# Two attentions and a soft mixture of experts on one core: one load stream through a byte ring, k turned on VectorE, second scores turned twice, and one written order for every part

## The chip, the cores and the metric

The kernel runs on one core of one Trainium2 chip, in fp32. The metric is the device time of one execution, in microseconds (us). A core has five engines that work side by side, each in the order of its own instructions: PE (TensorE, matmuls and transposes; its weight loads are shown apart, as PEld), DVE (VectorE), ACT (ScalarE), POOL (GpSimd) and SP (SyncE, which issues the transfers). Sixteen DMA engines carry the transfers between HBM and SBUF, the on-chip memory of 128 partitions. Matmuls write to PSUM, from where ACT or DVE copies.

## The reference

Eight batches, eight heads, 576 tokens, 64 values a head, and 32 packed queries `p` a head. Attention is done twice, then a soft mixture of eight experts with four slots each:

```
p_packed = softmax(scale * p @ k.T) @ v              # 32 x 64 for each batch and head
out      = softmax(scale * q @ p_packed.T) @ p_packed  # 576 x 64
x        = out as (4608 tokens, 512)
logits   = x @ phi                                   # 4608 x 32 slots
d = softmax of logits over the 4608 tokens;  slot_input = d.T @ x        # 32 x 512
slot_out[e] = relu(slot_input[e] @ w1[e]) @ w2[e]    # w1 512 x 1024, w2 1024 x 512
c = softmax of logits over the 32 slots;     result = c @ slot_out       # 4608 x 512
```

q, k and v are 9.4 MB each, the experts' weights 33.6 MB, the result 9.4 MB. The first-layer product of an expert needs slot inputs that depend on all tokens, so the experts come after the whole attention.

## The kernel before

**Steps.** The attention is cut into eight steps of two batches and four heads; two steps with the same batches make a duo. In a step `kp` (line 210) turns k on PE, 18 transposes of 128x128 into PSUM, copied to `kT` by `evac` (line 81, ACT or DVE, whichever has less to do by a running sum). `s1` (225) makes the scores of the packed queries, 16 matmuls that contract 64 rows, their maximum on DVE (247) and exponentials on ACT (251), which writes them with a stride of 18 elements so that keys 4p+j come together. `ap` (262) and `at` (277) turn these, `ppm` (285) multiplies with v, `ppn` normalises, `pt` (318) turns the packed values into `ppT`, `mp` (330) multiplies them with phi. `qp` (348) turns q, 18 transposes. `s2p` (367) makes the second scores with tokens on the partitions, 36 matmuls of 64 columns with q as the weights; `s2m`, `s2s` (386, 393) subtract the maximum on DVE, `e2` (424) is the exponential on ACT, `n2` (428) sums on DVE and scales on POOL, `a2p` (447) turns the result, `lg` (463) makes the logits. After each duo `f1` to `f4`, `gz`, `grg`, `gtg`, `gbg`, `gsg` (495 to 690) bring its share of the slot inputs to the running maximum.

**Order.** The loop at line 753 writes a turn by hand: step i to its scores, step i+1 to its packed keys. The last step and the last duo stand in a second hand-written order (line 867). Each engine follows its own instructions in that order.

**Loads.** All transfers go through SP's one queue. The big tiles of k, q, v and the weights share a pool of 15 places of 16 KB a partition (`NRING`); what does not fit lies in small tail tiles. k is loaded in rows of 4,096 bytes (line 111) and tails of 512 (112); q and v in rows of 1,024 bytes (121) and tails of 256 that go to 64 partitions (132). A w1 chunk is loaded by `load_w` (718) as two transfers of 512 KB, each to 64 of the 128 partitions, rows of 4,096 bytes (722, 723); a w2 chunk as one of 1 MB to all partitions, rows of 8,192 bytes (736). Pools for late weights open as attention tiles are given back (`extra`, `more`, `more2`, `more3`).

**Experts and result.** `layer1a` (line 978) runs four experts' first layers into one pair of banks in four column groups, `hidden` and `layer1b` turn the hidden units, `layer2` (1033) does the second layers (its matmul is line 1037), the last expert in halves of columns. The result is 36 matmuls of full contraction in fp32r (line 1150), copied by ACT and DVE, and written in 12 + 2 transfers.

## Time and profile before

| | |
|---|---|
| time, median of 3 runs | 259.22 us (255.44 to 261.7) |
| span of the profiled execution | 253.4 us |
| own time of the profiled execution, with what lies around the span | not listed apart; the fastest run is 2.0 us above the span, the median 5.8 us |
| busy PE, PEld, DVE, ACT, POOL | 200.2, 133.7, 119.7, 116.2, 25.0 us |
| mean granted clock of TensorE | 0.925 of full speed |
| bytes moved | 62.46 MB read, 9.44 MB written |

The span runs from the first to the last instruction. Busy time of PE is overlapped by its pipeline, so 145 us busy in 166 does not mean 145 us of columns. In the table by stretches each engine has its busy time and, in brackets, its instructions; PEclk is the granted clock as a share of full speed, and the DMA share is that of 16 engines.

### The profile page before, as it was taken

How to read it: one execution, taken by the hardware profiler on the slowest of the kernel's cores; microseconds unless marked ns; L12 is line 12 of the kernel's file. 1: busy time of each engine (PE TensorE's matmuls, PEld its weight loads, DVE VectorE, ACT ScalarE, POOL GpSimd, SP SyncE). 2: the span in 40 equal slices, each digit the busy share in tenths (PEclk: the TensorE clock that was granted, in tenths of full speed). 3: DMA queues.
4: the chain of work that ended last, by engine and by line, in shares of the span. 5: the costliest groups of instructions: out<-in, count | busy, mean ns of one | idle time of the engine just before them, and what ended most of it. 6: DMA issues, size and time to landing. Idle time of an engine off the chain costs nothing.

```text
span 253.4 us, 6754 instructions
## 1 busy us (share of the span) xinstructions
PE 200.2 (79%) x2843; PEld 133.7 (53%) x2843; DVE 119.7 (47%) x279; ACT 116.2 (46%) x253; POOL 25.0 (10%) x40
## 2 busy tenths in 40 slices
PE   1878899989979998879977976988462999989700
PEld 1556766756846866647845765754111433456300
DVE  2223463563853472785453535767710125168700
ACT  2385469577625669256658453451100200069700
POOL 3000003030030012021003003200020000000000
PEclk9999799999967999999999979899795899999965
DMA  5999999999999999999999999999999999039996
GB/s 153 304 312 278 320 285 301 260 319 291 294 308 313 320 303 288 241 239 262 284 256 240 244 235 349 420 341 208 223 229 290 398 416 379 21 109 398 419 411 156
DMA packets 41246, 72.33 MB, mean 285 GB/s; under 512 B 11392, under 2 KB 31104, under 8 KB 38400
## 3 DMA queue, kind: packets, MB, share of 16 engines
q1 hardware_dynamic: 41216, 71.90, 97.1%
q8 instruction: 22, 0.36, 0.6%
q14 instruction: 8, 0.07, 0.1%
HBM read 62.46 MB, written 9.44 MB: 284 GB/s over the span
## 4 chain that ended last, share of the span: by engine, by line
PE 54%; DMA 20%; ACT 12%; issue 5%; DVE 2%; SPq 1%; ACTq 0%
DMA w<-in_moe_w_dram 16%; PE s L380 7%; PE kp L220 7%; PE s L240 6%; PE so L1037 5%; PE hp L988 4%; PE m L294 4%; PE qp L361 4%; ACT a L251 4%; PE op L1150 2%; DMA k<-in_k_dram 2%; ACT kT L88 2%; ACT qT L88 2%; PE ap L269 2%; ACT a1T L88 2%
## 5 line engine op out<-in xcount | busy, mean ns | idle before, releaser
L88 ACT COPY kT<-kp 128x512 f32<-128x512 f32 (+1 forms) x42 | 19.1, 484 | 27.4 <-PE kp L220 27.4
L988 PE MATMUL hp<-w,xz 128*32 128x512 f32 x128 | 20.0, 675 | 10.9 <-DMA w<-in_moe_w_dram 10.4
L380 PE MATMUL s<-ppT,qT 128*64 128x64 f32 x576 | 22.6, 238 | 3.0 <-issue 1.9
L443 POOL TENSOR_TENSOR a<-a,z 128x1152 f32<-128x1152 f32 (+1 forms) x8 | 16.0, 1996 | 81.8 <-DVE z L442 62.3
L220 PE MATMUL kp<-ident,k 128*128 128x128 f32 x128 | 21.0, 307 | 3.6 <-issue 1.7
L380 PEld LDWEIGHTS s<-ppT,qT 128*64 128x64 f32 x576 | 20.2, 150 | 6.5 <-ACT qT L88 3.1
L88 ACT COPY qT<-qp 128x512 f32<-128x512 f32 (+1 forms) x40 | 20.3, 558 | 3.9 <-PE qp L361 3.4
L251 ACT ACTIVATE a<-s,nm 128x576 f32<-128x576 f32 x16 | 21.6, 1352 | 0.5 <-DVE nm L247 0.5
L220 PEld LDWEIGHTS kp<-ident,k 128*128 128x128 f32 x128 | 16.3, 157 | 8.8 <-issue 4.3
L247 DVE TENSOR_REDUCE nm<-s 128x1 f32<-128x576 f32 x16 | 12.0, 750 | 17.9 <-PE s L240 17.9
L390 DVE TENSOR_REDUCE mx<-s 128x16 f32<-128x512 f32 (+1 forms) x24 | 12.6, 555 | 16.2 <-PE s L380 16.1
L240 PE MATMUL s<-kT,pT 64*32 64x288 f32 x256 | 17.1, 446 | 3.8 <-ACT kT L88 3.3
L361 PE MATMUL qp<-ident,q 128*128 128x128 f32 x128 | 19.1, 286 | 0.9 <-issue 0.9
L88 ACT COPY a1T<-ap 128x512 f32<-128x512 f32 x16 | 8.7, 589 | 20.8 <-PE ap L269 20.8
L988 PEld LDWEIGHTS hp<-w,xz 128*32 128x32 f32 x128 | 6.4, 119 | 22.3 <-issue 21.4
L361 PEld LDWEIGHTS qp<-ident,q 128*128 128x128 f32 x128 | 16.0, 150 | 1.9 <-issue 1.9
L294 PE MATMUL m<-v,a1T 128*32 128x64 f32 x512 | 10.7, 232 | 4.5 <-issue 3.1
L435 DVE TENSOR_REDUCE z<-a 128x36 f32<-128x1152 f32 (+2 forms) x9 | 10.9, 1209 | 6.9 <-ACT a L426 6.2
L1037 PE MATMUL so<-w,hT 128*32 128x512 f32 x112 | 12.4, 592 | 0.0
L1005 ACT COPY hs<-hp 128x512 f32<-128x512 f32 x2 | 1.2, 586 | 24.4 <-PE hp L988 24.4
L294 PEld LDWEIGHTS m<-v,a1T 128*32 128x32 f32 x512 | 8.7, 116 | 6.6 <-issue 4.0
L1150 PE MATMUL op<-sh,cT 128*128 128x512 f32 x35 | 11.9, 444 | 0.2
(155 smaller groups left out, 321.3 us busy)
## 6 DMA issues: line engine op xcount, KB each, us to landing
w<-in_moe_w_dram SPq DMA_DIRECT2D x34, 512.0 KB, 16.4
w<-in_moe_w_dram SPq DMA_DIRECT2D x15, 1024.0 KB, 15.8
k<-in_k_dram SPq DMA_DIRECT2D x16, 512.0 KB, 6.7
q<-in_q_dram SPq DMA_DIRECT2D x16, 512.0 KB, 7.4
v<-in_v_dram SPq DMA_DIRECT2D x16, 512.0 KB, 8.0
out_dram<-ob SPq DMA_DIRECT2D x7, 1024.0 KB, 6.1
kx<-in_k_dram SPq DMA_DIRECT2D x16, 64.0 KB, 6.0
qx<-in_q_dram SPq DMA_DIRECT2D x16, 64.0 KB, 7.4
```

The lines of the kernel that those rows point to most:

```text
L88: nc.scalar.copy(dst, src)
L220: nc.tensor.transpose(tp[:, j * P : (j + 1) * P], src, ident)
L240: nc.tensor.matmul(ps[hs, x, 0:HALF], pTs[dd][xs, g, 4 * b2 + h].rearrange("p a s -> p (a s)"), kT[xs, :, hs], start=True, stop=True,)
L251: nc.scalar.activation(a1.rearrange("p (r t x) -> p x t r", t=T, x=2), ps[:, :, 0:HALF].rearrange("p x (t r) -> p x t r", t=T), AF.Exp, bi ...
L294: nc.tensor.matmul(s["m"][hs, b2 * D : (b2 + 1) * D], s["a1T"][:, 4 * b2 + j, hs] if j < 4 else a1tail[:, b2, hs], vm[:, b2, h, j * D : (j ...
L361: nc.tensor.transpose(tp[:, j * P : (j + 1) * P], qf[:, o : o + P], ident)
L380: nc.tensor.matmul(ps[us, j * 64 : j * 64 + 64], s["qT"][:, 8 * c + j, us], w, start=True, stop=True)
L390: nc.vector.tensor_reduce(mx, s[f"s2{c}"], axis=AX.X, op=ALU.max)
L443: eng.tensor_tensor(a2, a2, z2.unsqueeze(3).broadcast_to([P, nt, 4, NS]), op=ALU.mult)
L988: nc.tensor.matmul(hp[nh][32 * a : 32 * a + 32, :], xzf[:, (4 * e + a) * NSLOT : (4 * e + a + 1) * NSLOT], w1s[e, a // 2][:, a % 2, nh * 5 ...
L1037: nc.tensor.matmul(so[32 * a : 32 * a + 32, :], hTf[:, (NJ * e + j) * NSLOT : (NJ * e + j + 1) * NSLOT], w2s[e, j // 4][:, j % 4, :], star ...
L1150: nc.tensor.matmul(op, cT[:, o, :], sh, start=True, stop=True)
```

## The change

The kernel function is written anew. These parts matter:

- **Loads.** One list of transfers in the order of use, p, k, q, v of all steps, then w1, then w2, goes through one SBUF ring of 112 KB a partition, handed out in bytes. `release` is called after the last reader of a region is written, and `pump` then issues every next transfer that fits. k, q and v come as half steps of 590 KB to all 128 partitions, in rows of nine tokens, 2,304 bytes, without tails. w1 chunks are 1 MB to all 128 partitions, rows of 4,096 bytes. Seven weight chunks go into the attention's work space (`f_late`) and one into the space of the last probabilities (`f_lx`).
- **k** is turned by VectorE in 32x32 blocks, four transposes of 128x576 a step, and the first scores contract 32 rows at a time in a 4x4 tiling, 16 groups in four banks.
- **First softmax.** The exponentials are written with 32 contiguous elements; the product with v contracts 64 rows into 64 columns.
- **Second scores** are made with the packed keys as weights and q moving, so that the slots lie on the partitions; they are copied to SBUF and turned back by nine transposes a step (`st`); then maximum, subtraction in eight parts, exponential, sum on POOL (VectorE for the last step), scale.
- **The duo's share** is summed in column groups, `gr` in four, with tokens 64 at a time.
- **Result.** The slot shares stay in fp32, four tokens' slots side by side, and 36 matmuls contract 32 rows each.
- **Order.** Every part of the attention is one word of `ORDER`, 638 words, with its PSUM bank and the engine of its copy; the words `w` are matmuls of ones.

```diff
-NRING = 15
-NEXTRA = (2, 2, 2, 1, 1)
-NTAIL = 6
-NKTAIL = 3
-NAHEAD = 3
+RING = 28 * 4096
+NEXT = (3, 2, 2)
+ORDER = """
+p.0.0 w.4.0@0 w.1.0@0 px.0.0@4 kt.0.0 pc.0.0:a kt.0.1 kt.0.2
+kt.0.3 w.4.0@0 w.4.0@0 w.1.0@0 s1.0.0@0 s1.0.1 qp.0.0@7 mx1.0.0
+qp.0.2@6 qc.0.0:a qp.0.4@5 qp.0.3@4 qc.0.2:a qp.0.5@7 qc.0.4:v e1.0.0
...
+"""
...
-    def load_k(i):
-        dd, g = divmod(i, NG)
-        main = ring.tile([P, 2, 16 * D], F32, tag="ring", name=f"k_{i}")
-        tail = kpool.tile([P, 2, 2 * D], F32, tag="tail", bufs=NKTAIL, name=f"kx_{i}")
-        for b2 in range(2):
-            xs = k[2 * dd + b2, 4 * g : 4 * g + 4].rearrange("h (r t) d -> (h r) (t d)", r=32)
-            nc.sync.dma_start(out=main[:, b2], in_=xs[:, 0 : 16 * D])
-            nc.sync.dma_start(out=tail[:, b2], in_=xs[:, 16 * D : 18 * D])
-        kts[i] = (main, tail)
...
-        dd, g = divmod(i, NG)
-        main = ring.tile([P, 2, 4, TB * D], F32, tag="ring", name=f"{name}_{i}")
-        for b2 in range(2):
-            xs = src[2 * dd + b2, 4 * g : 4 * g + 4]
-            nc.sync.dma_start(
-                out=main[:, b2],
-                in_=xs[:, 0 : TB * P, :].rearrange("h (p j) d -> p h (j d)", j=TB),
-            )
-        return main
...
+    def region(key, width):
+        off = state["off"]
+        if off + width > RING // 4:
+            off = 0
+        state["off"] = off + width
+        return [key, off, width]
...
+    def pump():
+        while state["next"] < len(loads):
+            key, width, src = loads[state["next"]]
+            if key == "phi":
+                nc.sync.dma_start(out=width, in_=src)
+                state["next"] += 1
+                continue
+            if "at" not in state:
+                state["at"] = region(key, width)
+            _, off, _ = state["at"]
+            if not free(off, width):
+                return
+            regions.append(state.pop("at"))
+            where[key] = (off, width)
+            load(ring[:, off : off + width], src)
+            state["next"] += 1
...
+    def release(key, users=1):
+        left[key] = left.get(key, users) - 1
+        if left[key]:
+            return
+        for x in regions:
+            if x[0] == key:
+                regions.remove(x)
+                break
+        pump()
...
+    def rows9(src, i, b2):
+        dd, g = divmod(i, NG)
+        s = src[2 * dd + b2, 4 * g : 4 * g + 4]
+        return s.rearrange("(m x) (r t) d -> (x r) m (t d)", m=2, t=T)
...
+    for i in range(NSTEP):
+        for b2 in range(2):
+            loads.append((f"k{i}.{b2}", 2 * T * D, rows9(k, i, b2)))
...
+        for b2 in range(2):
+            loads.append((f"q{i}.{b2}", 2 * T * D, rows9(q, i, b2)))
+        for b2 in range(2):
+            loads.append((f"v{i}.{b2}", 2 * T * D, rows9(v, i, b2)))
...
+    def rows_w1(e, g):
+        return w1[e, 2 * P * g : 2 * P * (g + 1)].rearrange("(j p) f -> p j f", j=2)
+    LX = (3, 1)
+    for e in range(E):
+        for g in range(NG):
+            if (e, g) != LX:
+                loads.append((f"w1_{e}_{g}", 2 * FF, rows_w1(e, g)))
+    for e in range(E):
...
-    w1s, w2s = {}, {}
-    chunks = [(lay, e, c) for lay in (1, 2) for e in range(E) for c in range(2)]
-    def load_w(pool, lay, e, c):
-        n = f"w{lay}_{e}_{c}"
-            t = pool.tile([P, 2, FF], F32, tag="ring", name=n)
-            for g in range(NG):
-                nc.sync.dma_start(
-                    out=t[64 * g : 64 * g + 64],
-                    in_=w1[e, g * 4 * D : (g + 1) * 4 * D].rearrange("(h d) f -> d h f", d=D)[
-                        :, 2 * c : 2 * c + 2
-                    ],
-                )
...
-        for t0, nt in ((0, 4), (4, 4), (8, 1)):
-            tp = bank(pstr, f"kp_{i}_{b2}_{t0}")
-            for j in range(nt):
-                t = t0 + j
-                src = main[:, b2, t * P : (t + 1) * P] if t < 8 else tail[:, b2]
-                nc.tensor.transpose(tp[:, j * P : (j + 1) * P], src, ident)
-            evac(kT[:, t0 : t0 + nt].rearrange("p t x -> p (t x)"), tp[:, 0 : nt * P])
+    def f_kt(i, j, bank, eng):
+        b2, c = divmod(j, 2)
+        nc.vector.transpose(
+            kT[:, b2, :, c].rearrange("p m (t r) -> p m t r", t=T),
+            view(f"k{i}.{b2}").rearrange("p (m t c d) -> p m t c d", m=2, t=T, c=2)[:, :, :, c],
+        )
+        release(f"k{i}.{b2}", 2)
...
+    def f_s1(i, j, bank, eng):
+        dd, g = divmod(i, NG)
+        c = j
+        for y in range(4):
+            b2, m = y // 2, 1 - y % 2
+            for z in range(4):
+                rs = slice(32 * z, 32 * z + 32)
+                nc.tensor.matmul(
+                    ps[32 * y : 32 * y + 32, z, 0 : 32 * T],
+                    pT[rs, dd, b2, g, c, m],
+                    kT[rs, b2, m, c],
+                    start=(c == 0),
+                    stop=(c == 1),
+                )
...
+    def f_e1(i, x, bank, eng):
+        nc.scalar.activation(
+            a1[:, :, x].rearrange("p t (h r) -> p h t r", h=2),
+            s1v[:, x].rearrange("p h (t r) -> p h t r", t=T),
+            AF.Exp,
+            bias=nms[i % 2][:, x : x + 1],
+            scale=1.0,
+            accum_out=rzs[i % 2][:, x : x + 1],
+        )
...
+    def f_m(i, j, bank, eng):
+        if j == 0:
+            banks["m", i] = bank
+        b = banks["m", i]
+        for t in range(*tk(j)):
+            for b2 in range(2):
+                for x in range(2):
+                    rs = slice(64 * x, 64 * x + 64)
+                    nc.tensor.matmul(
+                        ps[64 * b2 : 64 * b2 + 64, b + x, 0:P].rearrange("p (m d) -> p m d", m=2),
+                        a1T[rs, t, b2],
+                        view(f"v{i}.{b2}").rearrange("p (m t d) -> p m t d", m=2, t=T)[rs, :, t],
+                        start=(t == 0),
+                        stop=(t == T - 1),
+                    )
+        release(f"v{i}.0", 3)
+        release(f"v{i}.1", 3)
...
+    def f_s2(i, j, bank, eng):
+        if j == 1:
+            banks["s2", i, 1] = bank
+            for b2 in range(2):
+                for x in range(2):
+                    nc.tensor.matmul(
+                        ps[64 * x : 64 * x + 64, bank, R * b2 : R * b2 + R],
+                        ppTs[i % 2][:, x, b2, 1:3].rearrange("p v s -> p (v s)"),
+                        qT[:, b2, 4, 64 * x : 64 * x + 64],
+                        start=True,
+                        stop=True,
+                    )
+            return
...
+        b2 = j // 2
+        for x in range(2):
+            for m in range(2):
+                n0, n1 = nk(2 * m)
+                for u in range(2):
+                    us = slice(64 * u, 64 * u + 64)
+                    a = 2 * x + (u + m) % 2
+                    nc.tensor.matmul(
+                        ps[
+                            32 * a : 32 * a + 32,
+                            banks["s2", i, 2 * u],
+                            4 * R * b2 : 4 * R * b2 + 4 * R,
+                        ].rearrange("p (n r) -> p n r", n=4),
+                        ppTs[i % 2][us, x, b2, 2 * (1 - m) + u],
+                        qT[us, b2, n0:n1, 64 * x : 64 * x + 64],
+                        start=True,
+                        stop=True,
+                    )
...
+    def f_st(i, j, bank, eng):
+        n0, n1 = nk(j)
+        for n in range(n0, n1):
+            o = (n - n0) * P
+            nc.tensor.transpose(
+                ps[:, bank, o : o + P], s2T[:, n].rearrange("p b r -> p (b r)"), ident
+            )
+        banks["st", i, j] = bank
...
+    def f_mx2(i, j, bank, eng):
+        n0, n1 = nk(j)
+        nc.vector.tensor_reduce(
+            mxs[i % 2][:, n0:n1].rearrange("p n a -> p (n a)"),
+            ps[:, banks["st", i, j], 0 : P * (n1 - n0)].rearrange("p (a s) -> p a s", s=NS),
+            axis=AX.X,
+            op=ALU.max,
+        )
...
+        for k in range(2):
+            if j == 1:
...
+                u = j // 2
+                t0, w = (u, 1) if k == u else (1 + u, 0)
+                dst = a2s[i // NG % 2][:, t0 : t0 + 7 : 2, i % NG].rearrange(
+                    "p n (x w) s -> p n x w s", x=2
+                )[:, :, :, w]
+                a, b, w = src[:, :, :, k], m[:, :, :, k], [P, 4, 2, NS]
+            nc.vector.tensor_tensor(dst, a, b.unsqueeze(len(w) - 1).broadcast_to(w), op=ALU.subtract)
...
+    def f_z2(i, c, bank, eng):
+        a, z = a2v(i, c), part(zss[i % 2], c)
+        if eng == "v":
+            nc.vector.tensor_reduce(z, a, axis=AX.X, op=ALU.add)
+            return
+        y, w = part(zt, c), NS // 2
+        nc.gpsimd.tensor_tensor(y, a[:, :, :, 0:w], a[:, :, :, w:NS], op=ALU.add)
+        while w > 2:
+            w //= 2
+            nc.gpsimd.tensor_tensor(
+                y[:, :, :, 0:w], y[:, :, :, 0:w], y[:, :, :, w : 2 * w], op=ALU.add
+            )
+        nc.gpsimd.tensor_tensor(z, y[:, :, :, 0], y[:, :, :, 1], op=ALU.add)
...
+    def f_a2p(i, j, bank, eng):
+        t0, t1 = tk(j)
+        for t in range(t0, t1):
+            o = (t - t0) * P
+            nc.tensor.transpose(
+                ps[:, bank, o : o + P],
+                a2s[i // NG % 2][:, t, i % NG].rearrange("p c s -> p (c s)"),
+                ident,
+            )
+        banks["a2p", i, j] = bank
...
+    def f_gr(dd, j, bank, eng):
+        banks["g", dd] = bank
+        wide = dd < ND - 1
+        for t in range(T):
+            for k in range(4) if t == T - 1 and not wide else (None,):
+                for b2 in range(2):
+                    rs = slice(64 * b2, 64 * b2 + 64)
+                    c, xs = (t % 4, slice(0, 2 * P)) if k is None else (k, slice(64 * k, 64 * k + 64))
+                    nc.tensor.matmul(
+                        ps[32 * c : 32 * c + 32, bank + b2, xs],
+                        d_[rs, t],
+                        a2s[dd % 2][rs, t].rearrange("p g c s -> p (g c s)")[:, xs],
+                        start=(t < 4),
+                        stop=(t + 4 >= T) if wide else (t == T - 1),
+                    )
...
+    def f_w(n, j, bank, eng):
+        nc.tensor.matmul(
+            ps[:, bank, 0 : P * n].rearrange("p (n c) -> p n c", n=n),
+            ones,
+            ones.unsqueeze(1).broadcast_to([P, n, P]),
+            start=True,
+            stop=True,
+        )
...
+    def f_late(i, j, bank, eng):
+        if "at" in state:
+            state["off"] = state.pop("at")[1]
+        for x in range(sum(NEXT[:i]), sum(NEXT[: i + 1])):
+            key, width, src = loads[state["next"]]
+            where[key] = (work[:, 2 * FF * x : 2 * FF * (x + 1)], width)
+            load(work[:, 2 * FF * x : 2 * FF * x + width], src)
+            state["next"] += 1
+        pump()
...
+    def f_lx(i, j, bank, eng):
+        key = f"w1_{LX[0]}_{LX[1]}"
+        where[key] = (a2f, 2 * FF)
+        load(a2f[:, 0 : 2 * FF], rows_w1(*LX))
+    fs = {n[2:]: f for n, f in locals().items() if n.startswith("f_")}
+    for tok in ORDER.split():
+        x, _, eng = tok.partition(":")
+        x, _, bank = x.partition("@")
+        n, i, j = x.split(".")
+        fs[n](int(i), int(j), int(bank) if bank else None, eng)
...
-        nc.tensor.matmul(op, cT[:, o, :], sh, start=True, stop=True)
-        evac(dst, op)
+        for t in range(T):
+            n4, a = divmod(dd * T + t, 4)
+            rs = slice(32 * a, 32 * a + 32)
+            b = obank[n % 8]
...
+            if n < 4:
+                if n == 0:
...
+            copy(eng, ob[:, t], ps[:, b])
+            n += 1
+            if t + 1 in ends:
+                nc.sync.dma_start(out=ov[:, t1 : t + 1], in_=ob[:, t1 : t + 1])
+                t1 = t + 1
+# ---- launch: one core; inputs and outputs as the reference has them ----
+_INS = ["q", "k", "v", "p", "moe_phi", "moe_w1", "moe_w2"]
```

## Rows read from the trace of the kernel before

**Rows 1.** The page's 40 equal slices: busy tenths, clock, DMA, GB/s.
```profile
PE   1878899989979998879977976988462999989700
...
PEclk9999799999967999999999979899795899999965
DMA  5999999999999999999999999999999999039996
GB/s 153 304 312 278 320 285 301 260 319 291 294 308 313 320 303 288 241 239 262 284 256 240 244 235 349 420 341 208 223 229 290 398 416 379 21 109 398 419 411 156
```

**Rows 2.** The chain that ended last, pieces in order: start, us, what.
```profile
153.95 22.07 DMA w<-in_moe_w_dram
...
176.03 18.50 DMA w<-in_moe_w_dram
...
194.66 5.43 PE hp L988 x32
...
208.79 10.30 PE so L1037 x96
...
223.28 0.38 ACT sh L1141
```

**Rows 3.** Stretches: length, busy us by engine (x instructions), clock, DMA share, GB/s.
```profile
core 0: us, PE busy (x) PEld busy (x) DVE busy (x) ACT busy (x) POOL busy (x), PEclk, DMA share, GB/s
9.00:175.00 166.00, 145.00 (x2461) 108.10 (x2461) 87.64 (x214) 96.28 (x218) 20.83 (x25) 0.95 1.06 290
20.00:70.00 50.00, 45.52 (x839) 34.11 (x838) 27.59 (x65) 32.92 (x74) 5.70 (x8) 0.97 1.07 296
21.25:23.75 2.50, 2.50 (x46) 1.26 (x39) 0.80 (x2) 0.82 (x4) 0.00 (x0) 1.00 1.14 361
87.00:92.00 5.00, 4.74 (x110) 3.82 (x106) 3.50 (x9) 3.23 (x7) 0.00 (x0) 1.00 1.10 329
104.00:140.00 36.00, 29.89 (x526) 22.14 (x527) 19.64 (x46) 22.46 (x50) 5.21 (x6) 1.00 1.05 255
154.00:168.00 14.00, 11.87 (x195) 9.10 (x190) 8.91 (x24) 5.17 (x14) 4.22 (x3) 0.88 1.00 410
175.00:196.00 21.00, 10.34 (x56) 3.41 (x60) 8.33 (x16) 1.16 (x1) 1.83 (x1) 0.81 1.03 241
197.00:213.00 16.00, 16.00 (x156) 6.32 (x152) 5.90 (x15) 2.25 (x4) 0.29 (x1) 0.97 0.99 408
229.00:247.00 18.00, 9.93 (x39) 5.16 (x38) 9.65 (x15) 9.39 (x17) 0.00 (x0) 0.87 1.01 415
```

**Rows 4.** Groups of VectorE's instructions by line and shape: busy us, mean ns.
```profile
L247 DVE TENSOR_REDUCE nm<-s 128x1 f32<-128x576 f32 x16 | 12.0, 750 | 17.9 <-PE s L240 17.9
...
L390 DVE TENSOR_REDUCE mx<-s 128x16 f32<-128x512 f32 x16 | 11.1, 692 | 16.2 <-PE s L380 16.1
...
L664 DVE TENSOR_TENSOR rb<-gr,hm 128x256 f32<-128x256 f32 x8 | 3.0, 417 | 0.0
...
L1024 DVE STREAM_TRANSPOSE hq<-ht 128x256 f32<-128x256 f32 x2 | 0.9, 450 | 4.9 <-PE ht L1016 4.9
...
L525 DVE STREAM_TRANSPOSE d<-dL 128x32 f32<-128x32 f32 x4 | 0.8, 193 | 0.0
```

**Rows 5.** Groups of POOL, ACT and VectorE: the scale, exponentials, a blocked product.
```profile
L443 POOL TENSOR_TENSOR a<-a,z 128x1152 f32<-128x1152 f32 x7 | 14.9, 2132 | 75.9 <-DVE z L442 56.3 <-PE kp L220 9.9 <-ACT a1tail L283 9.6
...
L251 ACT ACTIVATE a<-s,nm 128x576 f32<-128x576 f32 x16 | 21.6, 1352 | 0.5 <-DVE nm L247 0.5
...
L579 DVE TENSOR_SCALAR rw<-rep,w,zg 128x32 f32<-128x32 f32 x4 | 2.8, 696 | 0.9 <-ACT w L570 0.9
```

**Rows 6.** Groups of copies out of PSUM on ACT and VectorE.
```profile
L88 ACT COPY kT<-kp 128x512 f32<-128x512 f32 x28 | 15.9, 588 | 25.9 <-PE kp L220 25.9
...
L91 DVE COPY ob<-op 128x512 f32<-128x512 f32 x12 | 8.2, 688 | 0.7 <-PE op L1150 0.4
```

**Rows 7.** The chain again, pieces of one step of the attention.
```profile
93.32 1.15 PE kp L220 x9
...
100.29 1.15 PE s L380 x32
...
102.65 1.31 PE s L380 x40
...
106.74 1.14 PE m L294 x64
```

**Rows 8.** Stretches of 2 us around one fall of TensorE's clock.
```profile
70.00:72.00 2.00, 0.85 (x18) 0.27 (x16) 1.58 (x2) 0.40 (x2) 1.81 (x1) 0.95 1.11 314
72.00:74.00 2.00, 1.60 (x16) 0.72 (x16) 0.87 (x3) 0.00 (x0) 0.31 (x1) 0.50 1.03 268
```

More of the change, by code (lines that the diff above doesn't have):

```diff
@@ new lines, in pack_attention_soft_moe @@
+    pps = ctx.enter_context(tc.tile_pool(name="pps", bufs=1, space=bass.MemoryType.PSUM))
+    ps = pps.tile([P, 8, 512], F32, name="ps")
+    psf = ps.rearrange("p b x -> p (b x)")
+    ring = ringp.tile([P, RING // 4], F32, name="ring")
+    ones = const.tile([P, P], F32, name="ones")
+    nc.vector.memset(ones, 1.0)
+    regions = []
+    loads = []
+    where = {}
+    state = {"next": 0, "off": 0, "out": 0}
+    def region(key, width):
[4 more added lines that the diff above has]
+        return [key, off, width]
@@ new lines, in view, with load, free @@
+    def view(key):
+        place, width = where[key]
+        return ring[:, place : place + width] if isinstance(place, int) else place[:, 0:width]
+    def load(dst, src):
+        shape = src.shape[1:]
+        if len(shape) == 2:
+            dst = dst.rearrange("p (a b) -> p a b", a=shape[0])
+        elif len(shape) == 3:
+            dst = dst.rearrange("p (a b c) -> p a b c", a=shape[0], b=shape[1])
+        nc.sync.dma_start(out=dst, in_=src)
+    def free(off, width):
+        return not any(o < off + width and off < o + w for _, o, w in regions)
@@ L225, in s1 @@
[L225 to L243 removed]
+    cm = const.tile([P, NT], F32, name="cm")
@@ L962, in pack_attention_soft_moe @@
[L962 to L994 removed]
+        elif dd < ND - 1:
+            nc.vector.tensor_tensor(S_run, S_run, bv, op=ALU.add)
@@ new lines, in pack_attention_soft_moe @@
+    des.close()
+    late2 = ctx.enter_context(tc.tile_pool(name="late2", bufs=1, reuse_waits="tile"))
+    hT = late2.tile([P, E, NJ * NSLOT + SPE], F32, name="hT")
+    nc.gpsimd.memset(hT, 0.0)
+    hTf = hT.rearrange("p e x -> p (e x)")
+    for e in range(QE):
+        layer1a(e)
+    for x in range(3):
+        f_cs(ND - 1, x, None, None)
+    hidden(0)
+    layer1a(QE)
+    layer1a(QE + 1)
+    layer1b(0)
+    layer1a(QE + 2)
+    layer1a(QE + 3)
+    hidden(QE)
+    layer2(0)
+    layer1b(QE)
@@ new lines, in pack_attention_soft_moe, with last2 @@
+    layer2(1)
+    layer2(2)
+    layer2(3)
+    f_cp(2, 0, 6, None)
+    f_cc(2, 0, None, "v")
+    layer2(4)
+    layer2(5)
+    layer2(6)
+    sot, so, sh = (a2f[:, x * DM : (x + 1) * DM] for x in range(3))
+    repf = rep.rearrange("p c s -> p (c s)")
+    def last2(j, x):
+        a = (j + 2 * x) % 4
+        nc.tensor.matmul(
+            ps[32 * a : 32 * a + 32, x, 0 : DM // 2],
+            hTf[:, (NJ * (E - 1) + j) * NSLOT : (NJ * (E - 1) + j + 1) * NSLOT],
+            w2v(E - 1, j)[:, halves[x]],
+            start=(j < 4),
+            stop=(j >= 4),
+        )
@@ new lines, in pack_attention_soft_moe @@
+    nc.vector.tensor_copy(sot, ps[:, SO])
+    for x in range(2):
+        for j in range(4):
+            last2(j, x)
+    for j0 in range(4, NJ, 2):
+        for x in range(2):
+            for j in range(j0, j0 + 2):
+                last2(j, x)
+    for x, xs in enumerate(halves):
+        nc.vector.tensor_tensor(so[:, xs], ps[:, x, 0 : DM // 2], sot[:, xs], op=ALU.add)
+    for x, xs in enumerate(halves):
+        nc.tensor.matmul(ps[:, 2 + x, 0 : DM // 2], repf, so[:, xs], start=True, stop=True)
```

1362 lines of the change are left out of this document (526 added, 836 removed).

## The prediction

> **What bounds the kernel now.** I read the page's slices first [rows 1]. The DMA line stands at 9 or more from the second slice to the 34th: the transfers never pause before 215 us, and yet their GB/s go from 208 to 420. So the queue is full, and what differs is the price of a byte. The chain comes next [rows 2]: it ends in 22.1 and 18.5 us of waiting for weights, from 154 to 194.5 us, although the attention itself is busy until 175; then PE runs through the experts (10.3 us for 96 second-layer instructions) and the result is written. Third, the stretches [rows 3], which put a rate to each kind of load: 296 GB/s while k, q and v come, 255 and 241 while w1 comes, 410 and 408 while w2 comes, 415 while the result goes out. The loads alone account for the end: k, q, v, p and phi are 28.9 MB, 98 us at 296; w1 16.8 MB, 67 us at 250; w2 16.8 MB, 41 us at 409; with 4 us of start 210 us. The attention stands beside it, from 9 to 175 us, with PE busy 145 of 166 us (0.87), ACT 96, DVE 88 [rows 3]; it delays the weights only where their place is still taken. Two limits lie close together, then: the stream, and the attention's order on its engines. A change must move both.
>
> **The loads, part by part.** The span of the new kernel is the end of its last load plus a tail, so the stream comes first.
> - k, q, v: rows of 2,304 bytes, no tails. No row has this size. The nearest are 329 GB/s (mostly q and v rows of 1,024 bytes, some tails) and 361 (k rows of 4,096 with small tails) [rows 3]; the upper end is 409 for 8,192. The tails that spoil both are gone, so I take 375: 28.9 MB are 77 us, bounds 71 and 98 (nothing gained).
> - w1: rows stay 4,096 bytes, but the target becomes 128 partitions instead of 64. The k rows of 4,096 bytes to 128 partitions ran at 361 even with tails [rows 3], so the row size is not what holds w1 at 250. I take 400: 42 us, bounds 41 and 67. [...]
> - w2: 41 us as now.
>
> Together 160 us, and with 3.5 us of start the stream could end at 164 us if it never waited (157 to 210).
>
> **When it waits.** The ring holds 112 KB, some four steps. A following transfer goes out when its region's last reader is through: by the written order the last q and v and the first weight chunk after word 250 of 638, fifteen w1 chunks by the end of q in step 7 (525), w2 of experts 0 to 2 by word 605, then the one chunk of `f_lx`, which waits for the last `gr`. The second layers of experts 3 to 7, 10.5 MB, follow only as first-layer products free the ring. So the last load ends no sooner than the start of the experts, T, plus 1 us, plus half of the `f_lx` chunk and 10.5 MB at 409 (27 us): T + 28. It decides if T is above 136.
>
> **What sets T.** The edits move work from PE to VectorE.
> - PE loses 18 transposes of k a step (2.3 us, two pieces of 9 at 1.15 [rows 7]) and most of the second scores (2.46 us now, 72 instructions; 40 now at 64 to 256 columns, about 1.1). It gains nine transposes `st` (1.15), and the product with v runs in 2x2 instead of four column groups: 72 instructions of 128 columns, where 64 of 64 columns took 1.14 us [rows 7]; about 1.9. The first scores stay near 1.2. By these about 10 to 11 us a step and 3 us a duo, some 95 us.
> - ACT loses most k copies (28 of 588 ns, 16 us [rows 6]) and gains those of `sc`. Its 16 exponentials at 1,352 ns for 576 columns [rows 5] write with a stride; now they write runs of 32. A 512-column copy costs 588 ns [rows 6], so 0.7 is near; unchanged, 10 us more. About 91 us.
> - VectorE: a block transpose cost 193 ns for 32 columns and 450 for 256 [rows 4], 1.15 ns a column, so 0.82 us for 576. Bounds: 0.75, a reduction of 576 columns [rows 4], and 1.35, the strided exponential [rows 5]. I take 0.82, the same operation: 32 are 26 us (24 to 43). First maxima 8 x 2 x 0.75 = 12; second maxima 16 x 0.69 and small ones, 13; subtractions 32 of 256 columns at 0.42 and 16 small ones, 17; some 30 copies of up to 0.69 [rows 6], 17; the four duos 16, slot shares 6, small ones (reciprocals, p, packed values) 19. Sum 126 us, against 88 now [rows 3]: VectorE becomes the busiest engine.
> - POOL takes the sums beside the scale: 2.13 us [rows 5] for 1,152 columns, and about 2.6 for halves that shrink; some 5 us a step of 13, hidden beside it. Not quite free: four small products on VectorE took 2.8 us together, 696 ns apiece [rows 5], against 0.42 for a wider one [rows 4]; they stand where POOL works. Bound 0 to 20 us on VectorE; instructions that overlap at their ends give back about as much as I expect (7), so I add nothing.
>
> Of the 126 us some 22 belong to the last step's softmax and the last duo, a chain of about 24 short parts of 0.3 to 1.3 us, 20 us. The other 104 us run from 7 us (k's first half) on. With the share that PE reaches in 20 to 70 us now, 45.5 of 50 [rows 3], they need 115: T = 7 + 115 + 20 = 142 (131 if VectorE never waits, 166 at a share of 0.75).
>
> **The sum.** Last load at 142 + 28 = 170 us; landing 2; last products, sum over groups and the copy `sh` 3 (4.2 now from the end of the 96 second-layer instructions to `sh` [rows 2]); from `sh` to the end 30.1 us now, of which 22.7 are 9.44 MB at 415 [rows 3]; the transposes between the first result tiles are gone there, 28.5. Span 203.5 us, against 253.4. The median of the runs stands 5.8 above the span shown, the fastest run 2.0; I add 4.5: **208 us**.
>
> **Rivals.**
> - *The new order is not dense* (chance 0.22). VectorE in order waits for PE and ACT as ACT does now (96 of 166 busy). At a share of 0.75, T = 166 and the span 227; with slow strided transposes too, a little more: 218 to 236 us. For it: 0.87 is the best of a whole attention now. Against: more steps are open at a time in the written order.
> - *The rates do not rise* (0.09). w1 stays at 250 and the rest at 296: the stream ends at 209, span 242.5, 247 us. With w1 alone unmoved 185 + 3.5 + 33.5 = 222, 226 us. Against: the k rows at 361.
> - *The stream sets all* (0.06): all loads at 409 and T below 128 give 157 + 33.5 = 190.5, 195 us.
> - *The other side: TensorE's clock falls through the attention* (0.05). [...] PE's 95 us at half clock are up to 190, so T could reach 7 + 190 + 20 = 217, span 278. It decides, against 253.4, from T = 192 on, a mean clock near 0.58. Against: the slices show 9 in nearly all of the attention [rows 1], even where PE is at 0.8. [...]
> - *The change does not do what it says*: a `pump` that always waits. It would show as a DMA line below 9 in the first half. It ends at the same T + 28 and lies in the first rival.
>
> **How the numbers follow.** The forecast, 196 to 218 us, has 0.56, the others as given, 0.02 for something slower than before. The range takes in the forecast and most of the first rival, 196 to 232, which leaves out a little of that, the unmoved rates, the fast end and the clock: 0.2. Two per cent, about what a measurement of this kernel can tell from no change, is 254 to 264.4 us. Below 254 lie all cases but the clock and a bad end of the order: faster 0.92, same 0.03, slower 0.05.
>
> **What would show it.** Right: w1 above 380 GB/s, k, q and v at 350 or more; VectorE busy near 125 us before the first product with w1, its block transposes near 0.8 us; first product with w1 at 135 to 150; the last load some 28 us after; PE without long waits in the experts; 31 us from the last load to the end. Wrong: the DMA line below 9 during the attention (the ring holds it back), block transposes above 1.2 us, a clock of 0.5 for whole steps, or an output stretch longer than now, because the 32-row products in fp32 or their copies lag behind the writes.

## Result and the profile after

The changed kernel takes **204.15 us** (median of 4 runs, 203.66 to 204.75), the kernel before 259.38 (4 runs, 255.44 to 261.7): ratio 0.7936, 95% interval 0.7866 to 0.8006, so 53 us less (55 between the medians). The forecast was 208 in a range of 196 to 232. The profiled execution took 204.49 us, its span 202.2 (before 253.4). Ratios here and below leave out slow executions, those more than 1.5% above the fastest of their kernel; the profiled executions of `e1` and `e3` are such slow ones, and the times of both are read from the other runs.

The page's slices, as [rows 1] shows them of before:

```profile
PE   7977986799899878899989999898999998798000
...
DVE  1688797679789999989947679588411211289000
...
PEclk9999999789999999999999999999999999999655
DMA  6999999999999999967879999989599998089997
GB/s 216 375 389 346 388 397 389 391 388 392 388 390 389 390 388 391 412 224 277 295 267 367 405 412 417 417 314 401 192 417 423 423 423 333 6 324 414 410 419 300
```

A slice is 5.1 us. GB/s stands at 388 to 397 from 20 to 81 us, while k, q and v come, where [rows 1] had mostly 260 to 320, and above 400 for most of the weights, where it had 208 to 284 for w1. The DMA line now falls below 9 in four slices from 86 to 106 us: the ring holds the stream back. The same in stretches, as [rows 3]: k, q and v; w1; the pause; w1 again, from about 125 us with the first of w2; w2; the result; and last the attention up to the first product of the experts.

```profile
core 0: us, PE busy (x) PEld busy (x) DVE busy (x) ACT busy (x) POOL busy (x), PEclk, DMA share, GB/s
5.00:68.00 63.00, 55.20 (x1038) 39.39 (x1044) 51.87 (x116) 35.19 (x85) 15.50 (x22) 0.97 1.05 385
80.00:86.00 6.00, 5.20 (x90) 3.55 (x78) 5.87 (x14) 4.48 (x13) 1.60 (x1) 1.00 1.03 412
86.00:110.00 24.00, 22.94 (x489) 17.47 (x489) 19.42 (x53) 16.68 (x43) 5.39 (x6) 1.00 0.80 281
110.00:131.00 21.00, 19.98 (x281) 13.85 (x265) 16.11 (x43) 13.88 (x33) 11.46 (x13) 1.00 1.03 413
146.00:170.00 24.00, 23.91 (x231) 8.14 (x225) 3.30 (x7) 1.17 (x2) 0.00 (x0) 1.00 1.00 416
182.00:199.00 17.00, 4.19 (x32) 2.64 (x26) 4.81 (x9) 5.31 (x11) 0.00 (x0) 0.68 1.02 413
7.00:142.00 135.00, 121.18 (x2235) 87.43 (x2234) 111.49 (x276) 81.56 (x204) 39.01 (x43) 0.99 0.99 371
```

The chain that ended last, pieces in order (start, us, what), from several stretches, to be read against [rows 2, 7]:

```profile
16.55 6.30 DMA ring<-in_v_dram
...
22.87 12.90 DMA ring<-in_k_dram
...
99.84 1.44 POOL zt L696
...
104.19 2.14 POOL work L711
...
106.92 1.31 PE ps L453 x9
...
124.55 2.14 POOL a L711
...
146.11 8.12 DMA ring<-in_moe_w_dram
...
154.29 18.77 DMA ring<-in_moe_w_dram
173.10 0.65 PE ps L1109 x8
```

It has three parts. Up to 35.8 us it waits for loads. From there to 142 us it goes through the engines in turn; summed over its pieces, VectorE has 43 us of it, TensorE 40, ScalarE 9, GpSimd 8. From 146 to 173 us it waits for w2. The first product of the experts (L1005) is at 142.4 us; I call it T, as the prediction does. Last, groups of instructions by line (busy us, mean ns), for the terms of the sum, beside [rows 4 to 7]:

```profile
L408 DVE STREAM_TRANSPOSE work<-ring 128x576 f32<-128x576 f32 x32 | 23.4, 756 | 4.3 <-DMA ring<-in_k_dram 3.7
...
L475 PE MATMUL ps<-ring,work 64*64 64x128 f32 x576 | 17.9, 273 | 0.7 <-ACT work L358 0.7
...
L436 ACT ACTIVATE work<-ps,nm 128x576 f32<-128x576 f32 x16 | 11.8, 744 | 4.8 <-DVE nm L433 4.8
...
L881 PE MATMUL ps<-ones 128*128 128x512 f32 (+2 forms) x30 | 12.7, 542 | 1.0 <-DVE ones L149 1.0
L422 PE MATMUL ps<-work 32*32 32x288 f32 x512 | 13.4, 425 | 0.0
...
L634 PE MATMUL ps<-ident,work 128*128 128x128 f32 x72 | 12.3, 288 | 0.0
```

### The profile page after: what moved, and what is told of

It reads as the page before. It is cut to its first block, busy times and chain, and to the rows that moved or that the text cites. A ratio compares the mean times of both kernels' runs of the same rounds, so it can differ in the third digit from the quotient of the medians.

```text
span 202.2 us, 6267 instructions
## 1 busy us (share of the span) xinstructions
PE 168.7 (83%) x2633; PEld 107.5 (53%) x2633; DVE 131.0 (65%) x315; ACT 96.0 (47%) x232; POOL 46.0 (23%) x72
## 4 chain that ended last, share of the span: by engine, by line
DMA 30%; PE 24%; DVE 22%; ACT 7%; issue 5%; POOL 4%; SPq 0%; ACTq 0%; DVEq 0%; POOLq 0%
DMA ring<-in_k_dram 14%; DMA ring<-in_moe_w_dram 13%; DVE work L408 4%; PE ps L566 3%; DMA ring<-in_v_dram 3%; ACT ring L358 3%; DVE mx L641 3%; DVE a L670 2%; PE ps L720 2%; PE ps L607 2%; PE ps L634 2%; PE ps L453 2%; PE ps L422 2%; PE ps L1005 2%; DVE nm L433 2%
## 5 line engine op out<-in xcount | busy, mean ns | idle before, releaser
L358 ACT COPY work<-ps 128x512 f32<-128x512 f32 (+3 forms) x91 | 40.3, 479 | 28.5 <-PE ps L566 9.8
L408 DVE STREAM_TRANSPOSE work<-ring 128x576 f32<-128x576 f32 x32 | 23.4, 756 | 4.3 <-DMA ring<-in_k_dram 3.7
L566 PE MATMUL ps<-ident,ring 128*128 128x128 f32 x144 | 21.9, 287 | 0.3 <-ACT work L358 0.2
L566 PEld LDWEIGHTS ps<-ident,ring 128*128 128x128 f32 x144 | 16.3, 144 | 4.5 <-issue 1.8
L475 PE MATMUL ps<-ring,work 64*64 64x128 f32 x576 | 17.9, 273 | 0.7 <-ACT work L358 0.7
L475 PEld LDWEIGHTS ps<-ring,work 64*64 64x64 f32 x576 | 15.6, 133 | 3.4 <-issue 1.3
L641 DVE TENSOR_REDUCE mx<-ps 128x16 f32<-128x512 f32 (+1 forms) x24 | 13.0, 545 | 1.8 <-PE ps L634 1.7
L881 PE MATMUL ps<-ones 128*128 128x512 f32 (+2 forms) x30 | 12.7, 542 | 1.0 <-DVE ones L149 1.0
L422 PE MATMUL ps<-work 32*32 32x288 f32 x512 | 13.4, 425 | 0.0
L1005 PE MATMUL ps<-ring,a2Tb 128*32 128x512 f32 x96 | 12.4, 594 | 0.0
L634 PE MATMUL ps<-ident,work 128*128 128x128 f32 x72 | 12.3, 288 | 0.0
L453 PE MATMUL ps<-ident,work 128*128 128x128 f32 x72 | 10.3, 279 | 1.2 <-ACT work L436 1.1
```

Source lines behind the costliest of these rows:

```text
L358: nc.scalar.copy(dst, src)
L408: nc.vector.transpose(kT[:, b2, :, c].rearrange("p m (t r) -> p m t r", t=T), view(f"k{i}.{b2}").rearrange("p (m t c d) -> p m t c d", m=2 ...
L422: nc.tensor.matmul(ps[32 * y : 32 * y + 32, z, 0 : 32 * T], pT[rs, dd, b2, g, c, m], kT[rs, b2, m, c], start=(c == 0), stop=(c == 1),)
L453: nc.tensor.transpose(ps[:, bank, o : o + P], a1[:, t].rearrange("p x r -> p (x r)"), ident)
L475: nc.tensor.matmul(ps[64 * b2 : 64 * b2 + 64, b + x, 0:P].rearrange("p (m d) -> p m d", m=2), a1T[rs, t, b2], view(f"v{i}.{b2}").rearrange ...
L566: nc.tensor.transpose(ps[:, bank, o : o + P], view(f"q{i}.{b2}")[:, P * n : P * n + P], ident)
```

## The experiments

The first three ask which part of the change gave what; the others ask what sets T and the end.

**w1 in two halves, in the kernel after** (`e1`):

```diff
-            load(ring[:, off : off + width], src)
+            if key.startswith("w1"):
+                for y in (0, 64):
+                    load(ring[y : y + 64, off : off + width], src[y : y + 64])
+            else:
+                load(ring[:, off : off + width], src)
```

(and the same for w1 chunks that go to other places).

> The new kernel with each w1 chunk loaded as two transfers of 512 KB to 64 partitions each, the same rows of 4,096 bytes, the same bytes to the same places. If the half target holds w1 back (my theory), w1 falls from about 415 to about 250 GB/s: 16.8 MB cost 27 us more, of which the pause of the stream between 86 and 110 us hides some 8; the first products then meet late chunks, and the time rises by 12 to 20 us, to 216 to 224 us. If only the length of the rows counts (rival), nothing changes: 203 to 205 us.

Measured 225.22 us in the fastest run, 21 more than the kernel after, and 231.53 to 232.54 in the other three. A stretch of w1, the longest wait of the chain and three shorter ones, all from the run of 232.54:

```profile
110.00:150.00 40.00, 33.12 (x433) 23.45 (x432) 24.74 (x69) 21.58 (x55) 13.68 (x14) 0.96 1.04 235
```

```profile
92.47 2.80 issue
...
110.02 3.45 issue
...
120.02 2.19 issue
...
152.10 23.63 DMA a<-in_moe_w_dram
```

The theory's direction holds; even the fastest run lies past the upper end of its size. w1 comes at 235 GB/s, and the chunk that goes into the last probabilities' space, which can be issued only when those are done, holds TensorE until 175.9 us. T is 155.1 us instead of 142.4, although every load of the attention is issued before the first of w1 (69.1 us): on the way TensorE pauses three times for nothing that the profile shows (`issue`), which `e2` takes up. There is no trace of the fastest run, so how much of this delay it shares stays open. The row length is the same 4,096 bytes in both kernels. The transfers are also half as large, 512 KB, but that is not it: k in the kernel before came in transfers of that size and rows of that length to 128 partitions, at 361 GB/s even with small tails between [rows 3], and `e7` below moves still smaller ones at 347. So the half width of the target does it: 235 GB/s with it, 412 and 413 in the kernel after.

**w1 in full width, in the kernel before** (`e2`):

```diff
-            for g in range(NG):
-                nc.sync.dma_start(
-                    out=t[64 * g : 64 * g + 64],
-                    in_=w1[e, g * 4 * D : (g + 1) * 4 * D].rearrange("(h d) f -> d h f", d=D)[
-                        :, 2 * c : 2 * c + 2
-                    ],
-                )
+            nc.sync.dma_start(
+                out=t, in_=w1[e, 2 * P * c : 2 * P * (c + 1)].rearrange("(j p) f -> p j f", j=2)
+            )
```

> The kernel before with each w1 chunk loaded by one transfer of 1 MB to 128 partitions instead of two of 512 KB to 64; the rows of w1 then meet other slot inputs than they should, so the output is not the reference's. My theory: w1 at 400 GB/s or more, 26 us of transfers saved, but the attention still ends at 175 us: the first products need no more waits, PE works 29 us, and the time falls to 236 to 248 us. Rival, the rows of 4,096 bytes are slow in themselves: 256 to 262 us. Rival, the stream was not what decided: also unchanged, with w1 at 400.

Measured 225.11 us (224.46 to 226.65), ratio to before 0.8791 (0.868 to 0.8901): 31 us less, and 11 below the better end of what was expected. Where [rows 3] had 255 from 104 to 140 us:

```profile
100.00:130.00 30.00, 28.74 (x542) 21.93 (x538) 20.40 (x49) 19.97 (x45) 4.97 (x5) 1.00 1.04 370
130.00:160.00 30.00, 27.55 (x503) 20.84 (x502) 21.78 (x63) 17.08 (x45) 4.47 (x4) 1.00 0.96 374
```

The weights no longer wait, and the experts start at 160.9 us instead of 175.2. That was not in the expectation: the slow w1 had delayed the attention too. Some tails of q and v do stand behind w1 chunks in the queue of the kernel before, but between 90 and 165 us the profile shows no wait of TensorE for one. What it does there is stand still four times for 1.3 us or more, 6.6 us in all, for nothing that the profile shows; three of these stand in the chain of the kernel before:

```profile
112.52 1.71 issue
...
128.98 1.32 issue
...
145.60 1.73 issue
```

Each of the four ends 1.4 to 1.6 us after a load of 16 KB of instructions has ended (here the first of them, from 111.33 to 112.68 us). That TensorE waits here for its own instructions, late beside the slow transfers, is my reading of these times; no run shows it. Behind the last two pauses the granted clock fell to 0.50, for 3.4 us each. With w1 in full width TensorE has no such pause between 90 and 165 us, and its clock stays at 1.00. Of the 14.3 us by which the experts start sooner, 2.8 are there before the first chunk of w1 is issued, at 93 us, and are not w1's.

**k turned by VectorE, in the kernel before** (`e9`; blocks arranged otherwise, so the scores are not the reference's), and both of the last two (`e11`):

```diff
-        for t0, nt in ((0, 4), (4, 4), (8, 1)):
-            ...
-            evac(kT[:, t0 : t0 + nt].rearrange("p t x -> p (t x)"), tp[:, 0 : nt * P])
+        nc.vector.transpose(kT[:, 0:8].rearrange("p t x -> p (t x)"), main[:, b2])
+        nc.vector.transpose(kT[:, 8], tail[:, b2])
```

> The kernel before with k turned by VectorE in 32x32 blocks (1,152 columns for each batch and step) instead of 18 transposes on PE and their copies a step, in the old order; the blocks lie otherwise than the scores need, so the output is not the reference's. PE loses 26 us, ACT and VectorE 23 us of copies, VectorE gains about 22 us. If two limits lie close together (my theory), the attention ends 8 to 18 us earlier, but w1 still comes at 250 GB/s and the time falls little: 250 to 258 us. Rival, the attention's end decides alone: 241 to 250 us.

> The kernel before with both single changes: w1 by transfers to 128 partitions and k turned by VectorE, old order, old places; the output is not the reference's for both reasons. If both limits have to move, this falls by more than the two alone together: 222 to 236 us. If the effects merely add up, it is the sum of the two. If the order of the parts is what counts, it stays above 236 us.

Alone: 249.08 to 263.1 us in ten runs, beside 253.25 to 263.26 in thirteen of the kernel before, no difference that can be told. With w1 in full width: 221.59 (221.13 to 224.01), ratio 0.8693 (0.8582 to 0.8803), 3.5 below `e2`, whose runs don't overlap with these. So k on VectorE is worth little, 3.5 us once the stream is out of the way. Whether it is worth as much without that, and so whether the two merely add up, `e9` can't tell. Both together come to 17 us above the kernel after.

**Rows of 1,024 and 1,280 bytes for k, q, v, in the kernel after** (`e7`):

```diff
+                dv = ring[:, off : off + width].rearrange("p (m x) -> p m x", m=2)
+                for xs in (slice(0, 4 * D), slice(4 * D, T * D)):
+                    nc.sync.dma_start(out=dv[:, :, xs], in_=src[:, :, xs])
```

> The new kernel with k, q and v loaded in two transfers per half step, rows of 1,024 and 1,280 bytes in place of 2,304. If row length sets the rate of the attention's loads, it falls from 390 to 330 to 350 GB/s and the 28.3 MB take 9 to 13 us longer; the stream runs behind from the first step and the pause at 86 to 110 us hides about 8 of it: 204 to 209 us. Rival: the rate stays at 390 because the tails were what was slow before: 203 to 205 us and 385 GB/s or more in 20 to 65 us.

Measured 209.79 us (208.86 to 210.68), ratio to before 0.8182 (0.8102 to 0.8262): 5.6 above the kernel after, just past the upper end of the theory.

```profile
7.00:68.00 61.00, 49.02 (x990) 34.95 (x982) 46.00 (x108) 32.15 (x79) 13.61 (x16) 0.97 1.05 347
```

347 GB/s, where the kernel after has 387 in this stretch. The transfers are smaller too, 256 and 320 KB instead of 576, so row length and size are not told apart. The block transposes of the fourth step begin at 39.58 us instead of 35.87, and T is 146.6 instead of 142.4: what the loads lose in the first 40 us is kept to the end.

**A ring of 96 KB instead of 112** (`e10`):

```diff
-RING = 28 * 4096
+RING = 24 * 4096
```

> The new kernel with a ring of 96 KB a partition instead of 112. If the end is the start of the experts plus the weights that found no place before it, two more chunks (2.1 MB) come after it at 416 GB/s: 5 us more, 208 to 211 us, with the start of the experts unchanged within 1 us. If the whole stream alone sets the end (rival), it has pauses to spare: under 2 us more. If the attention waits for its loads with less run-ahead, the experts start later as well and it is more than 211.

Measured 210.56 us (210.2 to 212.87), as the theory had it, with T at 141.4. The end moved, not the start of the experts. From T to the last landing it takes 4.2 us more, as is to be expected with fewer weights on the chip at T. The rest comes behind it: the granted clock is at 0.50 from 173.4 to 180.2 us, and the last products, 32 instead of 8 behind the last wait, take 3.66 us instead of 0.65.

**What sets T.** Half of k's block transposes left out (`e3`), half of the first scores' contraction and four of nine tiles of the product with v left out (`e4`), and both (`e12`), each from step 1 on:

```diff
+        ms = slice(0, 2) if i == 0 else slice(0, 1)
         nc.vector.transpose(
-            kT[:, b2, :, c].rearrange("p m (t r) -> p m t r", t=T),
+            kT[:, b2, ms, c].rearrange("p m (t r) -> p m t r", t=T),
...
+        if c and i:
+            return
...
+            if t % 2 and i:
+                continue
```

> The new kernel with the block transposes of k at half their columns from step 1 on (288 of 576; the other half of k keeps what step 0 left, so the output is not the reference's). VectorE loses 28 times 0.3 to 0.38 us, about 10 us. If VectorE sets the end of the attention (my theory), the experts start 6 to 9 us earlier and the time falls to 195 to 199 us. If PE sets it (rival), they start at most 2 us earlier: 202 to 204 us.

> The new kernel with less work on PE from step 1 on: the first scores contract only the first half of the head's values, and the product with v takes five of nine token tiles, so the output is not the reference's. PE loses 7 times 0.9 and 7 times 1.1 us, about 14 us. If VectorE sets the end of the attention (my theory): 201 to 204 us. If PE does (rival): the experts start 8 to 12 us earlier, 192 to 197 us.

> The changed kernel from step 1 on with half of k turned by VectorE (half the width of each block transpose), half of the contraction of the first scores and five of the nine token tiles of the product with v left out: less on VectorE and on TensorE together (8.7 and 9.3 us less before T, as the two earlier experiments that leave out one each showed). Alone, the first moved the time from 204.2 to 201.9 and the second to 204.7. Theory (two engines at 0.90 and 0.83 of the stretch before T limit each other: relief of one runs into the other): together T falls by 6 to 10 us, time 194 to 198 us. Rival (neither sets T; the loads of the first steps and the dependences through the steps do): 201 to 204, no lower than the less on VectorE alone.

Measured 200.9 us (200.67 to 202.83, and 205.37 in the profiled run), 204.69 (204.54 to 206.57) and 201.36 (200.74 to 203.08). The first gave 3.3 us of the 5 to 9 expected, the second nothing, both together no more than the first. No theory by the sum of one engine's work stands, and the one by two engines failed as well, though not cleanly; the rival of `e12` has its number right. Three stretches and one piece of the chain of `e12`, from a run of 203.08, above its median:

```profile
7.00:140.79 133.79, 115.39 (x1789) 80.60 (x1788) 103.52 (x279) 81.84 (x204) 39.42 (x44) 0.95 1.00 377
...
102.00:104.00 2.00, 0.63 (x4) 0.41 (x5) 0.38 (x2) 1.71 (x6) 1.31 (x1) 0.91 1.00 403
104.00:106.00 2.00, 2.00 (x11) 2.00 (x11) 1.41 (x6) 1.10 (x4) 0.00 (x0) 0.50 1.01 406
```

```profile
104.05 2.03 PE ps L456 x9
```

At 93 us `e12` is 3.1 us ahead (the 36 products for the slots at 90.44, in the kernel after at 93.56), at T only 1.6. Behind a stretch in which TensorE was busy 0.63 of 2 us the granted clock fell to 0.50, and nine transposes took 2.03 us instead of 1.31 at 1.00. At this place, work taken from TensorE is given back in part by its clock. Over the whole way from 7 us to T the mean clock is 0.95, and 0.96 in `e4`, where it was 0.99; but it is 0.96 in `e3` too, which takes nothing from TensorE, so the mean alone does not show the cause.

**The second softmax's sums on VectorE instead of GpSimd** in steps 0 to 6 (`e5`), and in steps 4 to 6 alone (`e6`), by words of the order:

```diff
-z2.4.0:p st.5.1@6 ...
+z2.4.0:v st.5.1@6 ...
```

> The changed kernel with the sums of the second softmax of steps 0 to 6 on VectorE instead of GpSimd (the last step has them on VectorE already). The trace of the changed kernel has GpSimd at 3.4 us for the sums of one step (1.43, three of 1.74 together, 0.24) and 2.13 for the product behind them, and such pieces stand in the chain that ended last at 97 to 106 us and again at 113 to 127 us. Theory (T, the first product of the experts, is set by the dependences through each step, of which GpSimd's sums are a link): the link becomes shorter, since VectorE adds 128x576 in less than GpSimd's 1.43 us; T falls by 3 to 8 us and the time to 196 to 201 us. Rival (VectorE's work sets T, 111.5 us busy of the 135 before T): some 9 us more on VectorE put T later, time 208 to 213. Second rival (neither): 203 to 206.

> The changed kernel with the sums of the second softmax of steps 4, 5 and 6 alone on VectorE: the pieces of GpSimd that stand in the chain that ended last between 97 and 127 us. Theory (the dependences through these steps set T): T falls by 2 to 5 us, time 199 to 202. Rival (VectorE's work sets T): some 4 us more on VectorE, time 205 to 209. Second rival (other links of the same length take over): 203 to 205. If it lies below 202, it is the better version.

Measured 207.1 us (206.44 to 208.14) and 208.35 (206.92 to 209.53), T at 146.0 and 146.7. The theory falls, though its link did become shorter: one reduction on VectorE takes 1.26 to 1.35 us where GpSimd took 3.4. Pieces of the chain of `e6`, to be read against the chain of the kernel after above:

```profile
101.27 1.26 DVE zs L693
...
108.58 1.33 PE ps L453 x9
...
114.91 1.35 DVE zs L693
...
122.64 1.26 DVE zs L693
...
128.81 2.14 POOL a L711
```

The same nine transposes stand at 108.58 instead of 106.92, the same product of GpSimd at 128.81 instead of 124.55. VectorE went through its instructions as the order has them: the sum, and its wait for the exponential (1.4 us of idle time in `e6`), now stand ahead of the subtractions and maxima that TensorE and ScalarE wait for. Some 4 us of work on VectorE in these steps came out as 4.3 at T. The rival foresaw this side, and the time of `e6`; `e5` lies just under its range. But `e5`, with seven sums moved instead of three, lost no more, which speaks for the place rather than the sum. Its busy time on VectorE up to T grew by 5.1 us only (`e6`: 3.9), though its sums take 9.4: with GpSimd's sums gone, VectorE's small instructions of three lines (L487, L490, L770) took 149, 162 and 170 ns instead of 263, 369 and 452, 3.7 us less in all.

**Without the matmuls of ones** (`e8`): every word `w` taken out of the order.

> The changed kernel without the 30 matmuls of ones (12.7 us of TensorE over the span, their output read by nothing) that stand where TensorE would pause. Theory (they only keep the granted clock up, and lie beside the loads): without them the granted clock of the stretches at the start and behind the last attention step falls from 0.99 towards 0.5, and products there take twice their duration; since the end is the last load plus 2.9 us of products, and T is reached by a chain with few products of full width in it, the time is 204 to 209. Rival (they stand in TensorE's way, which was busy 121 of the 135 us before T): time 199 to 203. Rival (the clock before T falls for good): above 212.

Measured 206.97 us (205.54 to 207.71), 2.8 more; T at 143.7.

```profile
3.00:10.00 7.00, 4.25 (x80) 1.48 (x80) 3.24 (x6) 0.59 (x1) 3.04 (x19) 1.00 1.02 378
...
140.00:145.00 5.00, 3.86 (x34) 2.31 (x38) 2.97 (x10) 0.95 (x3) 1.77 (x1) 0.50 0.80 272
145.00:150.00 5.00, 5.00 (x40) 1.38 (x36) 1.29 (x4) 0.14 (x1) 0.06 (x1) 0.74 0.35 97
```

The theory is half right. At the start the clock stays at 1.00 without them. Shortly before T it falls to 0.50, from 127.1 to 130.5 us and from 137.4 to 147.6, the first products with w1 take up to 1,063 ns instead of 592, and so the ring frees later.

The times of the profiled executions side by side (us; the landing is the end of the chain's last wait for weights):

| kernel | T | last weights landed | landed less T | span |
|---|---|---|---|---|
| after | 142.4 | 173.1 | 30.7 | 202.2 |
| `e3`, k at half width | 143.8 | 174.5 | 30.7 | 203.6 |
| `e4`, less on TensorE | 144.3 | 175.0 | 30.7 | 204.8 |
| `e12`, both | 140.8 | 171.5 | 30.7 | 201.3 |
| `e5`, sums on VectorE | 146.0 | 177.0 | 31.0 | 206.1 |
| `e6`, three of them | 146.7 | 177.4 | 30.7 | 206.5 |
| `e7`, short rows | 146.6 | 177.4 | 30.8 | 207.0 |
| `e8`, no matmuls of ones | 143.7 | 176.3 | 32.6 | 205.4 |
| `e10`, ring of 96 KB | 141.4 | 176.3 | 34.9 | 208.4 |

No experiment that computes all of the reference came out faster than the kernel after.

## Why the prediction was right, and where it was not

- **The rates** were right, each a little low. k, q and v ran at 385 (375 taken), w1 at 412 (400), w2 at 416 (409). That w1's target width was the cause, read from one stretch of k rows [rows 3], is shown from both sides: 31 us less in the kernel before, 21 more in the kernel after. It is more than half of the gain of 53; the prediction costed it at 25 us (67 to 42) and did not see that it delayed the attention as well. k on VectorE adds 3.5; the other 17 come with the stream, its rows, the ring and the order together. Of single parts of that, the longer rows and larger transfers of k, q and v are worth 5.6 and 16 KB of ring 6.4, by `e7` and `e10`; the order was not taken apart.
- **When it waits** was right: the last load at T + 28 and 2 for the landing. Seven of nine kernels have it landed at T + 30.7 to 31.0. The two others are those in which the weights on the chip at T, or the rate at which products free them, was changed. The ring did hold the stream back near 90 us, the sign that I had called wrong; it does not upset a count from T, in which the size of the ring already stands.
- **What sets T** is the step that failed, although its number, 142, came out at 142.4. It was the sum of VectorE's work, "the busiest engine", by a share of 0.91. Before T, VectorE is busy 111.5 of 135 us (0.83) and TensorE 121.2 (0.90): TensorE is busier, and neither sum sets T. VectorE's 126 us were too much: the block transposes took 0.756 us (0.82 taken; 23.4 us in all, 26), the subtractions 14.7 (17), and the copies and small parts the rest of the difference. TensorE's 95 were too little: `st` took 12.3 us, 1.54 a step (1.15); the product with v 17.9, 2.24 a step (1.9); the first scores 13.4, 1.68 a step (1.2); the matmuls of ones, 6.9 from 7 to 142 us, had no term at all. These are 16 of the 26 us; the rest is not accounted for. A sum too large and a share too high cancelled, by luck. What the runs show in its place: loads up to 36 us (`e7` moves T by 4.2), and then one chain through four engines in an order that is written out, in which 4 us put in at the wrong place cost 4.3 (`e6`), while with 8.3 us less on VectorE and 6.2 less on TensorE from 7 us on T comes only 1.6 sooner (`e12`).
- **ScalarE and GpSimd.** 81.6 us before T (91 taken; the exponential with contiguous runs took 744 ns, as near to 0.7 as assumed). GpSimd's sums were costed at nothing, hidden beside the step. Those of one step stand in the chain, 3.3 us from 99.84 us on, and its products behind the sums twice, 2.14 us each; putting the sums on VectorE is dearer all the same. What they cost VectorE, also put at nothing, was at least the 3.7 us of `e5`.
- **The tail.** From the landing to the end of `sh` 2.4 us (3 taken), from there 26.7 (28.5), with the result at 413 GB/s. The time stands 2.3 above the span of the profiled execution (4.5 taken). With a landing 1 us later than forecast, these make the 4 us between 208 and 204.15.
- **The rivals.** The order was dense enough; the rates rose. The clock did not fall as in [rows 8]: 0.99 before T. Half the clock through the whole attention is in no run; from 7 us to T the mean is 0.95 in `e12`. By `e8` the matmuls of ones have a part in the 0.99 only shortly before T (0.50 without them, for 3.4 and 10.2 us), and in `e12`, where TensorE has less to do, the clock is at 0.50 from 104 to 106 us.

**Still open:** which links of the chain between 36 and 142 us would have to be shortened. The relief of one or two engines gave little, partly since the clock took some back (nine transposes 0.7 us longer in `e12`), so that the theory of two engines is not refuted for a clock that holds. A run that keeps TensorE's clock with matmuls of ones in the place of the work left out would tell; it was not made.

## What to carry to other kernels

Read a rate for each kind of load from a stretch of its own, and ask first whether its target spans all 128 partitions: here that alone was worth 31 of 53 us (370 and 374 GB/s in `e2` where there were 255). Where weights are freed by products, count the end from the start of those products (here T plus what is still off the chip): that held in seven of nine kernels here. A sum of an engine's work divided by a share can hit the right number for a wrong reason; before moving work to a less busy engine, see what stands behind that place in its queue.

## What the hardware showed that I had not expected

- Slow transfers to 64 partitions held up TensorE, which needed none of their data yet: beside w1 at 255 GB/s, TensorE of the kernel before stood still four times for 1.3 us or more, 6.6 us in all, each time until 1.4 to 1.6 us after a load of instructions had ended; with w1 in full width not once, and the experts started 14 us sooner, 11 of them gained beside w1.
- A block transpose on VectorE, 128x576 in fp32, takes 756 ns, about what a reduction of that width takes (750 [rows 4]), and 457 ns at half the width (`e3`).
- Less work on TensorE made its remaining work slower in places: nine transposes 2.03 us at a granted clock of 0.50 (`e12`) instead of 1.31 at 1.00; and 12.7 us of matmuls that nobody reads save 2.8 us (`e8`).
- Rows of 2,304 bytes moved at 385 GB/s, not much below rows of 4,096 at 412; rows of 1,024 and 1,280 at 347.
